# Weight splits of the first 14 chunks on GpSimd instead of ScalarE and VectorE

## Chip, core and metric

The kernel runs on one core of one Trainium2 chip. The core has five engines that run their own instruction queues side by side: TensorE (PE, matrix products), VectorE (DVE), ScalarE (ACT), GpSimd (POOL) and SyncE (SP, which here issues all transfers). The metric is the device time of one execution in microseconds (us); the median of several runs is compared.

## What is computed

Windowed attention over 8 batches and 8 heads (576 positions, 64 numbers per head), then a feed-forward layer with a PReLU in the middle, all float32:

```python
scores = q @ k.T / sqrt(64); masked to 32 positions (half of the heads: every 4th of 128)
attn = softmax(scores);  x = (attn @ v), laid out as 4608 tokens x 512
h = x @ w_in                                   # 512 x 2048
g = np.maximum(h, 0.0) + alpha * np.minimum(h, 0.0)
return g @ w_out                               # 2048 x 512
```

## The kernel before

Matrix products of the feed-forward layer run in a format with fewer bits (fp32r). To keep accuracy, each float32 operand is split in two: a **high** part, the number rounded to fp32r, and a **low** part, the number minus its high part. A product is then three matmuls: high by high, high weight by low activation, low weight by high activation (`PASSES`).

The weights `w_in` and `w_out` come in 32 chunks of 128x512 numbers (16 of each, mostly taken in turn: the list `wq`). The host hands them over as 8-byte numbers, so each chunk is put together on the chip first. The class `Conversion` does it, in steps that the schedule calls one by one:
- `magnitude()`: two instructions on ScalarE (L413, L414) make the tile `wa` (or a spare room with the name `w_2_dt.float_92` or `_93`).
- `words()`: two instructions on VectorE (L421, L423) put in the remaining bits. Both read two tiles in SBUF.
- `high()`: a copy on ScalarE (L429) rounds the chunk into its high part.
- `low()`: a subtraction on VectorE (L432) makes its low part.

The order of instructions on each engine is the order in which the program calls them; nothing reorders them, and each engine works its queue in order. The start of the program is an attention pipeline over pairs of heads (`pairs`), in which the first chunks are converted in the gaps. For one pair: `scores()` (PE, L222 and mask sums L232), `maxima()` (VectorE, L277, L281, later L274), `exponentials()` (ScalarE, nine instructions L287 with their sums), `divisions()` (VectorE, L294, L295 and L296, which multiplies the probabilities `pr` by the broadcast reciprocal sums `rs`, both in SBUF), `turns()` (VectorE transpose L302 into `pt`), `values()` (PE, L317 into `o`), `highs()` (ScalarE, L371) and `lows()` (VectorE, L376), which write high and low parts of the activations `x`. Between them stand a few matmuls on zeros, `idle()` (L126), with no use for the result. The helper `behind()` issues a transfer of one number of a tile, so that the loads after it in SP's queue wait for that tile.

From the fourth pair on, slices of the feed-forward layer of tokens 0 to 511 come in: `ffn_h` (PE, L444, needs the high and low part of a `w_in` chunk), ScalarE's L452, VectorE's L457, ScalarE's L470 (high part of `g`), VectorE's L475 (low part of `g`, from two tiles in SBUF) and `ffn_y` (PE, L492, needs a `w_out` chunk). Chunks 0 and 1 are needed first, by `ffn_h(0, 0, ...)` and `ffn_h(0, 1, ...)`.

GpSimd does nothing in this stage. Later it makes sums of weights in `combine` (L542 on 128x512, L545 on 128x256) while VectorE works on the feed-forward slices.

Of the kernel before, what the change touches and what calls it, by code (L numbers as in the profile page):

```python
# [8 lines left out]
F32 = mybir.dt.float32  # L9
# [25 lines left out]
NFP = NF // 2  # L35
AHEAD = 20
EARLY = 20
GP = 4
GF = 2 * GP
NRING = 10  # L40
# [26 lines left out]
def tile_window_attention_prelu_ffn(  # L67
# [12 lines left out]
    nc = tc.nc  # L80
# [19 lines left out]
    wS = dram.tile([NFP, 7, P, 2, 2 * P], F32, name="wS")  # L100
    wO = dram.tile([NF // GF, NC, GP, P, 2, 2, P], F32, name="wO")
    marks = dram.tile([2 * NC, 1], F32, name="marks")
# [31 lines left out]
    def weight(which, a, f):  # L134
        k = next(k for k in range(3) if f < SPANS[k][1])
        i = 2 * which + a
        if (i, k) not in places:
            places[i, k] = place(i, k)
        return places[i, k][:, f - SPANS[k][0], :]
# [254 lines left out]
    class Conversion:  # L394
# [31 lines left out]

        def high(self):
            self.dst = [weight(self.which, a, self.f) for a in range(2)]
            nc.scalar.copy(out=self.dst[0], in_=self.a.bitcast(F32))  # L429

        def low(self):
            nc.vector.tensor_tensor(  # L432
                out=self.dst[1], in0=self.a.bitcast(F32), in1=self.dst[0].bitcast(F32), op=ALU.subtract)


# [132 lines left out]
    for t in range(NSTD, NTILE, 2):  # L568
        for grp in range(NFP // GP):
            seq = []  # L570
            for i in range(GP):
                seq.append((i, 1))
                if i:
                    seq += [(i - 1, 3), (i - 1, 4)]
                seq += [(i, 7), (i, 6), (i, 2), (i, 5)]
            units += [wS[grp * GP + i, WBLOCK[q]].rearrange("p a n -> p (a n)") for i, q in seq]
            if (t, grp) in SEVENS:
                for i, q in YSTEPS:
                    if q == 0:
                        units += [wS[grp * GP + i, WBLOCK[q]].rearrange("p a n -> p (a n)") for q in (3, 4)]  # L580
                    elif q in YBLOCK:
# [48 lines left out]
    def token_parts(t):  # L630


        k0, k1, z0, z1 = raw(t, 0), raw(t, 1), raw(t + 1, 0), raw(t + 1, 1)

        def diff(out, x, y):
            return lambda: nc.vector.tensor_tensor(out=out, in0=x, in1=y, op=ALU.subtract)

        def high(name, x):
            return lambda: nc.scalar.copy(out=part_of(name, 0), in_=x)

        def low(name, x):
            return lambda: nc.vector.tensor_tensor(
                out=part_of(name, 1), in0=x, in1=part_of(name, 0).bitcast(F32), op=ALU.subtract)

        zeroth = [high("B11", k0), low("B11", k0), high("B21", k1), low("B21", k1)]
        first = [diff(k0, z0, k0), high("T1", k0), low("T1", k0)]
        second = [
            diff(z0, z1, z0), high("T3", z0), diff(k0, z1, k0), high("T2", k0), low("T3", z0),
            diff(k1, k1, k0), low("T2", k0), high("B22", z1), high("T4", k1), low("B22", z1), low("T4", k1),
        ]  # L650
        return zeroth, first, second
# [666 lines left out]
    for p in range(2 * NC, AHEAD):  # L1318
        n = EARLY + 2 * (p - 2 * NC)
        score_at[n] = pairs[p]  # L1320
# [164 lines left out]
```

## Time and profile before

| what | value |
|---|---|
| median of 3 runs | 857.62 us (856.12 to 858.17) |
| the profiled execution's own time | 858.02 us |
| its span | 855.9 us |
| busy in the span: PE, DVE, ACT, POOL | 836.5, 609.6, 435.1, 46.9 us |
| share of the span | 98%, 71%, 51%, 5% |

The span is what the profiler saw from the first to the last instruction; 2.12 us of the execution's own time lie around it. A share is an average over the whole program: PE has 19.4 us without work, and the question in each stage is what it waits for there.

### The profile page before, as it was taken

Reading aid. Unit: us, or ns where it says so; the run is one execution under the profiler, and the core shown is the slowest. Engines: PE = TensorE matmul, PEld = TensorE weight load, DVE = VectorE, ACT = ScalarE, POOL = GpSimd, SP = SyncE. Lnnn points to the kernel's source line nnn. Section 1 sums busy time; section 2 is a strip of 40 time slices with the busy share of each in tenths; the row PEclk is TensorE's granted clock in tenths of the full one; section 3 lists DMA queues with packets and bytes.
Section 4 is the critical chain, followed back from the end, with each engine's and each line's share of the span. In section 5 each row is a group of like instructions: output and inputs, shape, how many; then the busy total and the mean of one; then the engine's idle time right before and its main releaser. Section 6 shows DMA issues by size and latency. Waiting matters only on the chain.

```text
span 855.9 us, 20198 instructions
## 1 busy us (share of the span) xinstructions
PE 836.5 (98%) x8118; PEld 681.7 (80%) x8118; DVE 609.6 (71%) x1047; ACT 435.1 (51%) x1208; POOL 46.9 (5%) x52
## 2 busy tenths in 40 slices
PE   7889999999999999999999999999999999999998
PEld 5677888888888888887778888887888878888886
DVE  5987866766776768678647767777668958834983
ACT  6885766434334444555436543654356426633640
POOL 0000000200505340000000000000000000000000
PEclk9999999999999999999999999999999999999999
DMA  7852444026989963768876577769976776666774
GB/s 250 273 188 97 150 163 148 29 93 201 288 270 322 313 212 129 249 184 254 298 233 196 160 238 250 196 183 300 302 237 191 216 246 198 195 193 193 194 206 140
DMA packets 130746, 179.28 MB, mean 209 GB/s; under 512 B 9822, under 2 KB 74462, under 8 KB 130654
## 3 DMA queue, kind: packets, MB, share of 16 engines
q1 hardware_dynamic: 130654, 178.00, 66.9%
q8 instruction: 64, 1.05, 0.5%
q14 instruction: 28, 0.23, 0.1%
HBM read 136.02 MB, written 41.94 MB: 208 GB/s over the span
## 4 chain that ended last, share of the span: by engine, by line
PE 90%; DVE 4%; DMA 2%; ACT 1%; issue 1%; SPq 0%; ACTq 0%; DVEq 0%
PE h L444 16%; PE y L492 15%; PE pA L657 15%; PE y L909 15%; PE pC L657 7%; PE qA L1029 6%; PE pB L657 4%; PE o L317 3%; PE s L222 2%; PE qC L1029 2%; PE o L264 1%; PE qB L1029 1%; PE s L246 1%; DMA w_dt.float<-qT 1%; DMA v<-vX 1%
## 5 line engine op out<-in xcount | busy, mean ns | idle before, releaser
L444 PE MATMUL h<-x,w_dt.float32r 128*128 128x512 f32 x576 | 142.0, 396 | 0.9 <-ACT x L371 0.8
L492 PE MATMUL y<-g,w_dt.float32r 128*128 128x512 f32 x576 | 138.3, 389 | 0.0
L444 PEld LDWEIGHTS h<-x,w_dt.float32r 128*128 128x128 f32 x576 | 107.7, 189 | 24.0 <-ACT x L371 0.9
L492 PEld LDWEIGHTS y<-g,w_dt.float32r 128*128 128x128 f32 x576 | 108.0, 188 | 22.4
L287 ACT ACTIVATE pr<-pr,nm 128x64 f32<-128x64 f32 x216 | 72.3, 337 | 75.3 <-DVE nm L277 75.3
L470 ACT CAST g<-m 128x512 fp32r<-128x512 f32 x48 | 29.7, 619 | 74.8 <-DVE m L465 71.8
L657 PE MATMUL pA<-parts_w,ring_w 128*128 128x512 f32 x240 | 59.3, 389 | 0.0
L909 PE MATMUL y<-gp,ring_w 128*128 128x512 f32 x240 | 58.2, 394 | 0.0
L657 PE MATMUL pA<-parts_w,ring_xA 128*128 128x512 f32 x234 | 57.8, 389 | 0.0
L909 PE MATMUL y<-gp,ring_xA 128*128 128x512 f32 x228 | 54.9, 394 | 0.0
L657 PEld LDWEIGHTS pA<-parts_w,ring_w 128*128 128x128 f32 x240 | 45.1, 188 | 9.3
L909 PEld LDWEIGHTS y<-gp,ring_w 128*128 128x128 f32 x240 | 44.4, 188 | 9.4
L657 PEld LDWEIGHTS pA<-parts_w,ring_xA 128*128 128x128 f32 x234 | 43.9, 188 | 9.1
L909 PEld LDWEIGHTS y<-gp,ring_xA 128*128 128x128 f32 x228 | 42.2, 188 | 9.1
L475 DVE TENSOR_TENSOR g<-m,g 128x512 fp32r<-128x512 f32 x48 | 33.6, 700 | 15.5 <-ACT g L470 15.4
L699 ACT COPY stage<-pA 128x512 f32<-128x512 f32 x36 | 21.2, 589 | 44.1 <-PE pA L657 43.8
L464 DVE TENSOR_SCALAR m<-h,al 128x512 f32<-128x512 f32 x27 | 20.2, 749 | 29.8 <-PE h L444 29.8
L287 ACT ACTIVATION_READ_ACCUMULATOR pr<-pr,nm 128x1 f32 x216 | 40.7, 189 | 0.0
L713 ACT ACTIVATE n<-stage 128x512 f32<-128x512 f32 x51 | 32.3, 634 | 9.0 <-DVE stage L706 5.8
L793 DVE TENSOR_TENSOR gp<-stage,gp 128x512 fp32r<-128x512 f32 x48 | 32.1, 685 | 2.1 <-ACT gp L789 2.1
L717 DVE SCALAR_TENSOR_TENSOR n<-n,bal,stage 128x512 f32<-128x512 f32 x36 | 27.0, 749 | 6.9 <-ACT n L713 6.4
L725 DVE TENSOR_TENSOR gp<-n,gp 128x512 fp32r<-128x512 f32 x48 | 31.6, 683 | 0.0
(165 smaller groups left out, 1541.2 us busy)
## 6 DMA issues: line engine op xcount, KB each, us to landing
ring_w<-wS SPq DMA_DIRECT2D x67, 256.0 KB, 3.0
ring_xA<-wS SPq DMA_DIRECT2D x67, 256.0 KB, 3.0
ring_w<-wO SPq DMA_DIRECT2D x35, 256.0 KB, 3.0
ring_g<-wS SPq DMA_DIRECT2D x34, 256.0 KB, 2.9
ring_xA<-wO SPq DMA_DIRECT2D x34, 256.0 KB, 2.9
wO<-w_dt.float32r SPq DMA_DIRECT2D x32, 256.0 KB, 4.2
wS<-wc SPq DMA_DIRECT2D x16, 512.0 KB, 4.7
wy<-wO SPq DMA_DIRECT2D x32, 256.0 KB, 5.3
```

The source lines that it names most:

```text
L287: nc.scalar.activation(out=self.pr[:, r, :], in_=self.ps[r // CUT0][:, r % CUT0, :] if self.onto else self.pr[:, r, :], func=AF.Exp, bias= ...
L444: nc.tensor.matmul(ms[t, f], lhsT=weight(0, a, f)[:, c * P:(c + 1) * P], rhs=half(t, c)[:, e, :], start=(c == 0 and n == 0), stop=(c == NC ...
L470: nc.scalar.copy(out=g[:, 0, :], in_=ms[t, f])
L475: nc.vector.tensor_tensor(out=g[:, 1, :], in0=ms.pop((t, f)), in1=g[:, 0, :].bitcast(F32), op=ALU.subtract)
L492: nc.tensor.matmul(ys[t][c], lhsT=weight(1, a, f)[:, c * P:(c + 1) * P], rhs=g[:, e, :], start=(first and n == 0), stop=(last and n == 2),)
L657: nc.tensor.matmul(to, lhsT=w[:, (2 * a + c) * P:(2 * a + c + 1) * P], rhs=part_of(name, e)[:, c * TT:(c + 1) * TT], start=start and c == ...
L713: nc.scalar.activation(out=self.m[n], in_=self.at(n), func=AF.Relu, scale=-1.0)
L717: nc.vector.scalar_tensor_tensor(out=self.m[n], in0=self.m[n], scalar=bal[:, f:f + 1], in1=self.at(n), op0=ALU.mult, op1=ALU.add)
L725: nc.vector.tensor_tensor(out=g[:, 1], in0=self.m.pop(n), in1=g[:, 0].bitcast(F32), op=ALU.subtract)
L793: nc.vector.tensor_tensor(out=p[:, 1], in0=self.whole(n), in1=p[:, 0].bitcast(F32), op=ALU.subtract)
L909: nc.tensor.matmul(ys2[tt], lhsT=w[:, k * P:(k + 1) * P], rhs=g[:, e], start=j == 0 and n == 0, stop=j == GF - 1 and n == 2)
L1029: nc.tensor.matmul(named(to)[c], lhsT=w[:, b * P:(b + 1) * P], rhs=rhs[:, e], start=begins and k == 0, stop=i == GP - 1 and k == 2, skip_g ...
```

## The change

For chunks with an index below `ASIDE` = 14, `high()` is a copy on GpSimd (L431 of the changed kernel) and `low()` a subtraction on GpSimd (L436). The places of the calls in the program, and all other instructions, stay.

```diff
+ASIDE = 14
...
         def high(self):
             self.dst = [weight(self.which, a, self.f) for a in range(2)]
-            nc.scalar.copy(out=self.dst[0], in_=self.a.bitcast(F32))
+            if self.index < ASIDE:
+                nc.gpsimd.tensor_copy(out=self.dst[0], in_=self.a.bitcast(F32))
+            else:
+                nc.scalar.copy(out=self.dst[0], in_=self.a.bitcast(F32))
 
         def low(self):
-            nc.vector.tensor_tensor(
+            (nc.gpsimd if self.index < ASIDE else nc.vector).tensor_tensor(
                 out=self.dst[1], in0=self.a.bitcast(F32), in1=self.dst[0].bitcast(F32), op=ALU.subtract)
```

The changed kernel's lines stand one lower up to L427 and three to four lower behind it (L421 and L423 are L422 and L424 there, L296 is L297, L302 is L303, L376 is L377). On VectorE, in the iteration that ends with the probabilities of the second pair (`pt_1`), these rows stood before; `wa_0_207` is chunk 0, `wa_1_226` chunk 1, `wa_0_254` chunk 2:

```order
L421 SCALAR_TENSOR_TENSOR wa_1_226<-ws_1_108,wa_1_226 128x512
L423 SCALAR_TENSOR_TENSOR wa_1_226<-ws_1_108,wa_1_226 128x512
L432 TENSOR_TENSOR w_0_dt.float32r<-wa_0_207,w_0_dt.float32r 128x512
L277 TENSOR_REDUCE nm_2_341<-s_2_0_258 128x5
L277 TENSOR_REDUCE nm_2_341<-s_2_1_259 128x4
L281 TENSOR_SCALAR nm_2_341<-nm_2_341 128x9
L421 SCALAR_TENSOR_TENSOR wa_0_254<-ws_0_113,wa_0_254 128x512
L423 SCALAR_TENSOR_TENSOR wa_0_254<-ws_0_113,wa_0_254 128x512
```

In the changed kernel VectorE has, at the same place:

```order
L422 SCALAR_TENSOR_TENSOR wa_1_226<-ws_1_108,wa_1_226 128x512
L424 SCALAR_TENSOR_TENSOR wa_1_226<-ws_1_108,wa_1_226 128x512
L278 TENSOR_REDUCE nm_2_341<-s_2_0_258 128x5
L278 TENSOR_REDUCE nm_2_341<-s_2_1_259 128x4
L282 TENSOR_SCALAR nm_2_341<-nm_2_341 128x9
L422 SCALAR_TENSOR_TENSOR wa_0_254<-ws_0_113,wa_0_254 128x512
L424 SCALAR_TENSOR_TENSOR wa_0_254<-ws_0_113,wa_0_254 128x512
```

The low part of chunk 0 is gone from between the words of chunk 1 and the maxima of pair 2. On GpSimd, behind the instructions of the program's start, now stand (the names in front of the arrow are the places of the high and low parts):

```order
L431 CAST w_0_dt.float32r<-wa_0_207 128x512
L431 CAST w_0_dt.float32r<-wa_1_226 128x512
L436 ISA
L436 TENSOR_TENSOR w_0_dt.float32r<-wa_0_207,w_0_dt.float32r 128x512
L431 CAST w_0_dt.float32r<-wa_0_254 128x512
L436 TENSOR_TENSOR w_0_dt.float32r<-wa_1_226,w_0_dt.float32r 128x512
L431 CAST w_0_dt.float32r<-wa_2_370 128x512
L436 TENSOR_TENSOR w_0_dt.float32r<-wa_0_254,w_0_dt.float32r 128x512
L431 CAST w_0_dt.float32r<-w_2_dt.float_92 128x512
L436 TENSOR_TENSOR w_0_dt.float32r<-wa_2_370,w_0_dt.float32r 128x512
L436 TENSOR_TENSOR w_0_dt.float32r<-w_2_dt.float_92,w_0_dt.float32r 128x512
```

The low part of a chunk stands behind the high part of the next one, as it stood before on VectorE behind the words of the next one; the instruction `ISA`, which stood ahead of L542 in the kernel before, now stands ahead of the first subtraction. On ScalarE, the rows between the exponentials of pair 0 and those of pair 1 were

```order
L287 ACTIVATE w_2_dt.float_90,sums_79<-s_0_1_120,nm_0_210 128x64 x4
L429 CAST w_0_dt.float32r<-wa_0_207 128x512
L413 ACTIVATE wa_1_226<-ws_1_108 128x512
L414 ACTIVATE wa_1_226<-wa_1_226,least 128x512
L287 ACTIVATE w_2_dt.float_91,sums_80<-s_1_0_163,nm_1_229 128x64 x5
```

and L429 has left this place and the 13 others like it.

## Rows read from the trace of the kernel before

**Rows 1.** Stretches: length, busy PE, PEld, DVE, ACT, POOL; PE clock, DMA, GB/s.

```profile
18.00:73.00 55.00, 46.76 (x988) 35.83 (x981) 48.99 (x110) 45.33 (x175) 0.00 (x0) 0.97 0.63 213
73.00:164.00 91.00, 91.00 (x404) 75.33 (x403) 65.20 (x101) 56.32 (x96) 1.13 (x1) 1.00 0.35 121
```

**Rows 2.** PE in order of time: start, us, what, [idle before, what ended it].

```profile
23.22 1.35 PE L317 MATMUL o<-pt,w_dt.float 32*64 32x32 f32 x76 [1.05 <-DVE pt L302]
...
28.83 1.48 PE L317 MATMUL o<-pt,w_dt.float 32*64 32x32 f32 x76 [0.92 <-PE idle L126]
30.24 4.37 PE L444 MATMUL h<-x,w_dt.float32r 128*128 128x512 f32 x18
34.55 1.35 PE L317 MATMUL o<-pt,w_dt.float 32*64 32x32 f32 x76
...
48.02 1.70 PE L317 MATMUL o<-pt,w_dt.float 32*64 32x32 f32 x76 [2.18 <-issue]
49.65 4.19 PE L444 MATMUL h<-x,w_dt.float32r 128*128 128x512 f32 x12
...
66.00 1.35 PE L317 MATMUL o<-pt,w_dt.float 32*64 32x32 f32 x76 [1.34 <-issue]
```

**Rows 3.** By line: engine, what, count, ns (least/median/most), first and last start.

```profile
L429 ACT CAST w_dt.float32r<-wa x26: 602/610/692, 12.4 to 157.9; 128x512 fp32r<-128x512 f32 x26
L432 DVE TENSOR_TENSOR w_dt.float32r<-wa,w_dt.float32r x26: 648/685/696, 15.9 to 158.7; 128x512 fp32r<-128x512 f32 x26
L542 POOL TENSOR_TENSOR wsum_xB<-w_dt.float32r x4: 1289/1296/1297, 162.9 to 216.9; 128x512 f32<-128x512 f32 x4
L545 POOL TENSOR_TENSOR wsum_xB<-wsum_xB x8: 730/740/1125, 165.5 to 220.9; 128x256 f32<-128x256 f32 x8
```

**Rows 4.** VectorE in order of time, from chunk 2's words on.

```profile
18.93 0.73 DVE L421 SCALAR_TENSOR_TENSOR wa<-ws,wa 128x512 uint16<-128x512 uint16 x1 [1.40 <-ACT wa L414]
19.70 0.69 DVE L423 SCALAR_TENSOR_TENSOR wa<-ws,wa 128x512 uint32<-128x512 uint32 x1
20.31 0.88 DVE L376 TENSOR_TENSOR x<-o,x 128x288 fp32r<-128x288 f32 x3
...
21.55 0.76 DVE L296 TENSOR_TENSOR w_dt.float<-w_dt.float,rs 128x576 f32<-128x576 f32 x1
...
23.05 0.65 DVE L432 TENSOR_TENSOR w_dt.float32r<-wa,w_dt.float32r 128x512 fp32r<-128x512 f32 x1
23.61 0.81 DVE L277 TENSOR_REDUCE nm<-s 128x5 f32<-128x320 f32 x2
```

**Rows 5.** ScalarE in order of time, between two sets of exponentials.

```profile
16.92 0.66 ACT L429 CAST w_dt.float32r<-wa 128x512 fp32r<-128x512 f32 x1
17.43 0.71 ACT L413 ACTIVATE wa<-ws 128x512 f32<-128x512 bf16 x1
```

**Rows 6.** GpSimd and VectorE in order of time, where both work.

```profile
162.87 2.54 POOL L542 TENSOR_TENSOR wsum_xB<-w_dt.float32r 128x512 f32<-128x512 f32 x2 [162.43 <-PE h L444]
163.61 0.69 DVE L465 SCALAR_TENSOR_TENSOR m<-h,m 128x512 f32<-128x512 f32 x1
164.99 0.97 DVE L475 TENSOR_TENSOR g<-m,g 128x512 fp32r<-128x512 f32 x1 [0.69 <-ACT g L470]
165.49 3.28 POOL L545 TENSOR_TENSOR wsum_xB<-wsum_xB 128x256 f32<-128x256 f32 x4
```

**Rows 7.** VectorE in order of time: chunk 9's words, the last early divisions.

```profile
61.03 0.74 DVE L421 SCALAR_TENSOR_TENSOR wa<-w_dt.uint,wa 128x512 uint16<-128x512 uint16 x1
61.81 0.69 DVE L423 SCALAR_TENSOR_TENSOR wa<-w_dt.uint,wa 128x512 uint32<-128x512 uint32 x1
...
64.33 0.76 DVE L296 TENSOR_TENSOR w_dt.float<-w_dt.float,rs 128x576 f32<-128x576 f32 x1
```

**Rows 8.** A stretch with a lower PE clock, columns as in rows 1.

```profile
50.00:52.00 2.00, 2.00 (x6) 1.52 (x6) 1.97 (x5) 2.00 (x12) 0.00 (x0) 0.50 0.93 375
```

**Rows 9.** GpSimd's configuration instruction, columns as in rows 3.

```profile
L542 POOLq MODIFY_POOL_CONFIG  x2: 11/11/11, 0.7 to 0.8; - x2
```

## The prediction, made before the changed kernel ran

> **What bounds the kernel now.** I read the windows by stage first, since the page's shares average over stages. From 73 to 164 us PE works 91.00 of 91.00 us; from 18 to 73 us it works 46.76 of 55.00 [rows 1]. So whatever the change does there, PE's work behind 73 us only starts earlier or later by what happened before; all the profit must come out of the first 73 us, where PE lacks 8.24 us of work. VectorE has 48.99 us of work in the same 55 us and ScalarE 45.33 [rows 1]: these two feed the attention pipeline and PE waits for them. PE in order of time shows where: the values of a pair (L317) wait 1.05 us for `pt` at 23.22, 0.92 at 28.83, 2.18 at 48.02 and 1.34 at 66.00 [rows 2]; behind 66.00 no such wait is left. One more loss stands behind the wait before 48.02: the granted clock was 0.50 from 50 to 52 us, the lower of the two levels (1.2 GHz) [rows 8], and 12 matmuls took 4.19 us where 18 at 30.24 took 4.37, that is 2.91 for 12; with L317 at 1.70 us against 1.35 this is 1.28 + 0.35 = 1.6 us [rows 2]. The ceiling of any gain is then 8.24 + 1.6 = 9.9 us, 1.15%. About 0.3% (2.6 us) is what a measurement of this kernel can tell from no change.
>
> **What the change takes away.** 14 casts L429 of 0.61 us go from ScalarE and 14 subtractions L432 of 0.685 us from VectorE [rows 3], 8.5 and 9.6 us of busy time. On the path each is worth its distance to the next instruction: 17.43 - 16.92 = 0.51 us on ScalarE [rows 5] and 23.61 - 23.05 = 0.56 us on VectorE [rows 4]. Only those in front of 66.00 count, and only where that engine is what PE waits for.
>
> **What it adds.** GpSimd was idle in this stage [rows 1], so its own time costs nothing unless a weight comes late. The subtraction has the form of L542: two in 2.54 us, 1.27 each [rows 6]. The cast isn't in the trace. Two-input work took 1.296 us for 512 columns and 0.740 for 256 [rows 3], so 256 columns cost 0.556 us and 0.184 is fixed. The cast's bounds are 0.18 (the fixed part alone) and 1.30 (as dear as a subtraction). It reads one input of 512, as much as two inputs of 256 columns, so I take 0.74 and keep both ends.
>
> GpSimd's low parts follow its own queue, not VectorE's, and come at about the old time or earlier; the first matmuls that need them start at 30.24 [rows 2], while chunk 1's words were ready before the old L429 at 16.92 [rows 5]. Weights are therefore not late.
>
> **What it disturbs.** The trace shows that the two engines get into each other's way. L542 ran from 162.87 to 165.41. L475, which reads two tiles in SBUF, was issued at 164.99 and took 0.97 us, though L432, of the same form, takes 0.685 [rows 3, 6]; it ended at 165.96, 0.55 us after GpSimd. So all but the first 0.14 us of it stood still until GpSimd had finished. GpSimd suffers likewise: one L545 took 1.125 us instead of 0.740 [rows 3]. L465, with one input in SBUF and one in PSUM, kept its 0.69 us in the middle of L542 [rows 6]. I conclude that a VectorE instruction with two SBUF inputs waits for a running GpSimd instruction as a whole. In the attention pipeline these are L421, L423 and L296; L376, with one input from PSUM, should run on.
>
> Now one iteration. Chunk 2's words end at t = 19.70 + 0.69 = 20.39 [rows 4]. GpSimd starts 0.08 us behind what it waits for (165.41 to 165.49 [rows 6]), casts until t + 0.82, and its next instruction is chunk 1's subtraction, until t + 2.09. L296 was issued at 21.55 = t + 1.16 [rows 4] and could have gone on at t + 1.30. It is held until t + 2.09: 0.79 us late, and with it the transpose and PE's values. Against that stands the 0.56 us of the L432 gone. Each such iteration is 0.23 us worse.
>
> **The sum**, as shifts of the PE rows [rows 2]:
> - 23.22: chunk 2's words had waited 1.40 us for ScalarE [rows 4]. Two L429 in front of them are gone, so they come 2 x 0.51 = 1.02 us earlier; L296 is held 0.79: -0.23.
> - 28.83: -0.23 - 0.56 + 0.79 = 0.
> - 34.55: again +0.23. PE came to this straight from L444 without a wait, so a little of it may be covered; I take +0.2.
> - 48.02: two more L432 go, but one stood where VectorE waits for exponentials anyway; I count one. The divisions come late enough to miss GpSimd: +0.2 - 0.56 = -0.36.
> - 66.00: two chunks are converted in a row here. Chunk 8's cast becomes ready while L421 of 61.03 runs until 61.77 [rows 7]; GpSimd is next, until 62.51, and L423, which could have gone on at 61.81 + 0.14 = 61.95, is 0.56 late. Its end moves from 62.50 to 63.06, GpSimd casts chunk 9 until 63.88 and subtracts chunk 8 until 65.15. L296 (64.33, plus 0.56, minus 0.56 for the missing L432) could go on at 64.47 and is held 0.68. Sum: -0.36 - 0.56 + 0.56 + 0.68 = +0.32.
>
> PE has no wait behind 66.00 that could take this up, so the profiled execution's 858.02 us become 858.34. The median of the runs is 0.40 us lower, so the forecast is 857.9 us: no change. With the cast at 0.18 every hold is 0.56 shorter (one vanishes) and the shift at 66.00, with PE's own work as a floor at 34.55, comes to about -2.1, 855.5 us; with 1.30, and GpSimd going on to its subtraction without a break, to +3.15, 860.8 us.
>
> The Trainium skill (GPSIMD Engine Reference, 4.1 Engine selection) speaks against the change: elementwise work with two inputs is about twice as slow on GpSimd and belongs on VectorE; with one input it runs at about line rate. The trace agrees on the first half (1.296 against 0.685 us [rows 3]). Line rate at the page's 1.2 GHz would make the cast 0.43 us, an estimate, and by it the sum would be about -1.0 us instead of +0.32, 856.6 us.
>
> The Trainium skill (SBUF — State Buffer, Who interferes with whom) says further that VectorE's tensor_scalar from SBUF to SBUF can block in the same way. No run here shows it. L294 would then also wait, some 0.1 us in each of four iterations, an estimate, and the sum would be near +0.7 us.
>
> **The rivals.**
> 1. Faster: the holds mostly miss. L296 is issued while the cast still runs (cast over about 1.1 us) and takes the port before the subtraction, or the cast is so short that little is left. That L475 went ahead of L545 at 165.41 [rows 6] speaks for the first; against it, the two L542 followed each other without a gap. Without any hold the shifts are -1.02, then -1.58 (at 34.55 PE's own work sets it), -2.14 at 48.02 and -2.7 at 66.00: 854.9 us; if the wait at 48.02 is then short enough for the clock to stay up, 1.6 less, 853.3 us.
> 2. Slower: the cast costs about 1.2 us or more and GpSimd goes straight on to the subtraction. Place: L296 in four iterations, L423 at 61.81. The shift grows from +0.32 at 0.74 to +3.15 at 1.30, and passes 2.6 at about 1.18. Besides, PE's wait at 66.00 would grow past the 2.18 us after which the clock fell at 48.02; another 1.6 us gives 862.4. For it: GpSimd's two-input price. Against it: half the reads.
> 3. Slower: the instruction `ISA`, which becomes MODIFY_POOL_CONFIG, now comes behind chunk 1's cast, with the first subtraction right behind. Before, it ran at 0.7 us and took 0.011 us twice [rows 9], but whatever it started had until 162.87 to finish. Chunk 1's low part is needed by 30.24 + 6 x 0.243 + 0.49 = 32.2, and two subtractions and a cast take 3.3, so the first may start at 28.9; it could start at 16.92 + 0.74 = 17.7. Up to 11.2 us are hidden; a load of 20 us would give 866.
>
> **How the numbers follow.** The forecast, within 0.3% of before, gets 0.58, with a range of its own from 855.5 to 860; rival 1 gets 0.27, rival 2 0.11, rival 3 0.04. Faster is 0.27, same 0.58, slower 0.15. The range from 854.0 to 861.0 takes in most of rival 1 and of the cast's bounds, and leaves out the fall of the clock on top of rival 2, the late load, and rival 1 with the clock kept up.
>
> **What would show it.** PE rows of L317 should stand within 0.4 us of the old starts up to 66.00, and PE should stay without waits from there to 164. VectorE should lose 14 L432 but show its divisions at about 1.5 us instead of 0.76 in the iterations named, and one L423 near 1.25 us. GpSimd's cast should be near 0.74 us. The prediction is wrong if the divisions keep 0.76 us (rival 1), if the cast is over 1.1 us, if PE waits for GpSimd at `h`, or if the clock falls in another place than before: each gap near 2 us decides over 1.6 us.

## The result and the profile after

| | median | runs | mean granted clock of the runs |
|---|---|---|---|
| kernel before, beside it | 858.73 us (856.12 to 862.07) | 6 | |
| changed kernel | 864.03 us (861.78 to 865.50) | 6 | 0.9942 |

The changed kernel is slower: ratio 1.0058, 95% interval 1.0030 to 1.0085. The forecast was no change, 857.9 us, range 854.0 to 861.0. The profiled execution has a span of 863.0 us, 7.1 more than before.

I read the same stretches first. This is the view of windows of the changed kernel: the stage with the change, the next one, and two short stretches inside that the next paragraphs need. Columns: length, busy PE, PEld, DVE, ACT, POOL; PE clock, DMA, GB/s.

```profile
18.00:73.00 55.00, 43.08 (x961) 31.68 (x955) 45.48 (x94) 36.75 (x155) 16.57 (x17) 0.94 0.58 203
73.00:164.00 91.00, 91.00 (x397) 75.18 (x395) 62.23 (x99) 55.99 (x97) 8.37 (x8) 0.98 0.36 126
49.50:52.80 3.30, 3.30 (x4) 1.08 (x4) 2.49 (x7) 2.60 (x9) 0.00 (x0) 0.50 1.03 409
73.40:76.70 3.30, 3.30 (x9) 2.61 (x8) 2.31 (x7) 0.51 (x4) 1.67 (x2) 0.50 0.22 62
```

The two engines that were to be relieved are relieved: VectorE 48.99 to 45.48, ScalarE 45.33 to 36.75 us [rows 1]. PE nevertheless does 3.68 us less in the same 55 us, and behind 73 us it is busy without a break, as before. So all the loss is made ahead of 73 us or in the first microseconds behind it, and part of it at half the clock: the granted clock is 0.50 in the two short stretches here and from 25.6 to 28.9 us; before, it was in one stretch [rows 8]. PE in order of time shows where (start, us, what, [idle before, what ended it]):

```profile
22.97 1.35 PE L318 MATMUL o<-pt,w_dt.float 32*64 32x32 f32 x76 [1.26 <-DVE pt L303]
...
29.57 1.03 PE L318 MATMUL o<-pt,w_dt.float 32*64 32x32 f32 x52
31.83 0.55 PE L318 MATMUL o<-pt,w_dt.float 32*64 32x64 f32 x24 [1.24 <-issue]
32.31 4.38 PE L448 MATMUL h<-x,w_dt.float32r 128*128 128x512 f32 x18
36.62 1.35 PE L318 MATMUL o<-pt,w_dt.float 32*64 32x32 f32 x76
...
43.24 1.04 PE L318 MATMUL o<-pt,w_dt.float 32*64 32x32 f32 x54
47.80 0.54 PE L318 MATMUL o<-pt,w_dt.float 32*64 32x64 f32 x22 [3.52 <-issue]
48.27 1.21 PE L223 MATMUL s<-w_dt.float 64*32 64x64 f32 x72
49.41 3.67 PE L127 MATMUL idle<-pr 128*128 128x512 f32 x4
53.01 0.68 PE L318 MATMUL o<-pt,w_dt.float 32*64 32x32 f32 x29
...
71.60 1.49 PE L318 MATMUL o<-pt,w_dt.float 32*64 32x32 f32 x76 [2.78 <-issue]
73.02 4.60 PE L448 MATMUL h<-x,w_dt.float32r 128*128 128x512 f32 x12
```

Beside the old starts [rows 2] the values come 0.25 us earlier, then 0.74, 2.07, 4.99 and 5.60 us later. Behind the last one `h` takes 4.60 us at a granted clock of 0.50 instead of 3.02 (the same 12 matmuls at 63.08), 1.58 more: 5.60 + 1.58 = 7.18, the whole difference of the spans (7.1). What the reader should note besides: stops of PE marked "issue" stand in the middle of a group (52 matmuls, a stop, 24 matmuls; 3.52 us behind 44 us), where the profile shows nothing that is waited for. The step from 2.07 to 4.99 us lies around the stop of 3.52 us, and no VectorE instruction is held there; other profiles of the same work show 1.24 (e1) and 2.09 us (e12) at this place, so that step belongs in part to this execution. The 2.78 us ahead of the last values are marked "issue" too, but they end 0.10 us behind VectorE's transpose (L303, until 71.50): this is a wait for VectorE.

Now the question of the prediction: which VectorE instruction is held? VectorE in order of time, the first two iterations and the one of the last values:

```profile
16.46 1.26 DVE L282 TENSOR_SCALAR nm<-nm 128x9 f32<-128x9 f32 x1
...
19.80 1.21 DVE L295 TENSOR_SCALAR rs<-sums 128x9 f32<-128x9 f32 x1
...
21.30 0.76 DVE L297 TENSOR_TENSOR w_dt.float<-w_dt.float,rs 128x576 f32<-128x576 f32 x1
...
25.87 1.22 DVE L295 TENSOR_SCALAR rs<-sums 128x9 f32<-128x9 f32 x1
...
27.38 0.76 DVE L297 TENSOR_TENSOR w_dt.float<-w_dt.float,rs 128x576 f32<-128x576 f32 x1
...
67.70 1.18 DVE L295 TENSOR_SCALAR rs<-sums 128x9 f32<-128x9 f32 x1
...
69.17 1.52 DVE L297 TENSOR_TENSOR w_dt.float<-w_dt.float,rs 128x576 f32<-128x576 f32 x1
```

and GpSimd beside them:

```profile
15.75 0.62 POOL L431 CAST w_dt.float32r<-wa 128x512 fp32r<-128x512 f32 x1 [3.93 <-DVE wa L424]
16.41 1.28 POOL L436 TENSOR_TENSOR w_dt.float32r<-wa,w_dt.float32r 128x512 fp32r<-128x512 f32 x1
19.15 0.61 POOL L431 CAST w_dt.float32r<-wa 128x512 fp32r<-128x512 f32 x1 [1.46 <-DVE wa L424]
19.72 1.27 POOL L436 TENSOR_TENSOR w_dt.float32r<-wa,w_dt.float32r 128x512 fp32r<-128x512 f32 x1
25.23 0.61 POOL L431 CAST w_dt.float32r<-wa 128x512 fp32r<-128x512 f32 x1 [4.24 <-DVE wa L424]
25.80 1.27 POOL L436 TENSOR_TENSOR w_dt.float32r<-wa,w_dt.float32r 128x512 fp32r<-128x512 f32 x1
...
67.56 1.29 POOL L436 TENSOR_TENSOR w_dt.float32r<-w_dt.float,w_dt.float32r 128x512 fp32r<-128x512 f32 x1
68.81 1.25 POOL L436 TENSOR_TENSOR w_dt.float32r<-wa,w_dt.float32r 128x512 fp32r<-128x512 f32 x1
```

The multiplication L297, which the prediction named, keeps its 0.76 us in the first two iterations. Held is L295 in front of it, an addition to nine numbers per partition with one input (0.16 us otherwise, median over all 32). It was issued at 19.80, 0.08 us behind the start of the subtraction at 19.72, and ended at 21.01, 0.02 us behind the subtraction's end at 20.99; the same at 25.87, and with L282 (0.17 us otherwise) at 16.46. Ahead of the last values two subtractions follow each other, and two instructions are held: L295 by the first of them, about 1.0 us, and L297 by the second, 0.76 us.

### The profile page after: what moved, and what is told of

The parts are those of the page before. It is cut to its first block, busy times and chain, and to the rows that moved or that the text cites. A ratio compares the mean times of both kernels' runs of the same rounds, so it can differ in the third digit from the quotient of the medians.

```text
span 863.0 us, 20234 instructions
## 1 busy us (share of the span) xinstructions
PE 840.5 (97%) x8118; PEld 683.6 (79%) x8118; DVE 608.4 (71%) x1033; ACT 428.5 (50%) x1194; POOL 74.4 (9%) x80
## 4 chain that ended last, share of the span: by engine, by line
PE 89%; DVE 4%; DMA 2%; ACT 2%; issue 1%; SPq 0%; ACTq 0%
PE h L448 16%; PE y L496 15%; PE pA L661 15%; PE y L913 14%; PE pC L661 7%; PE qA L1033 6%; PE pB L661 4%; PE o L318 3%; PE qC L1033 2%; PE s L223 2%; PE o L265 1%; PE qB L1033 1%; PE s L247 1%; DMA w_dt.float<-qT 1%; PE idle L127 1%
```

## The experiments

Theory P (the port): the holds of VectorE by GpSimd's subtractions are the loss. Rivals: C, the falls of PE's clock; I, PE's stops for its instructions; D, work that comes earlier on VectorE and ScalarE does harm by itself. Each run is compared with the kernel before on the same chip.

**The changed kernel again, and its halves.** The first is the changed kernel itself. The second leaves the subtractions on VectorE, the third leaves the casts on ScalarE.

```diff
# e2, in low()
-            (nc.gpsimd if self.index < ASIDE else nc.vector).tensor_tensor(
+            nc.vector.tensor_tensor(
# e3, in high()
-            if self.index < ASIDE:
+            if False:
```

> The changed kernel as it is, once more. Port theory (VectorE waits for whole GpSimd instructions, and the short tensor_scalar of the divisions waits first): the same seven holds of 0.5 to 1.1 us on L282, L295 and L297 in front of the last early values, time again about 0.6% over before. Supply theory (PE stops in the middle of a pair's values, 1.2, 3.5 and 0.5 us, because its instructions are late, and this has nothing to do with GpSimd's port): the holds are there too, but the stops in PE have other lengths in this execution, and the time scatters by some 3 us with them.

Measured: 862.40 us, 1.0046 (1.0029 to 1.0063), mean clock 0.9947 where the kernel before had 0.9980 over its 29 runs. The loss repeats; L295 takes 1.03 to 1.17 us at three places, and L297 1.55 and 1.52 us at two.

> Only the 14 casts on GpSimd, the subtractions on VectorE as before. Port theory: a cast of 0.61 us that starts 0.08 us behind the words ends while VectorE is in L377, which doesn't need the port, so no hold over 0.2 us; ScalarE is 0.51 us lighter per chunk; time 0 to 1.5 us below before. Supply theory: PE's stops stay as in the changed kernel, time 2 to 6 us above before.

Measured: 859.86 us, 1.0009 (0.9994 to 1.0025), clock 0.9965. No L295 is held; one L424 takes 0.94 us instead of 0.69.

> Only the 14 subtractions on GpSimd, the casts on ScalarE as before. Port theory: a subtraction now starts behind ScalarE's cast, not behind the words, so it meets other VectorE instructions: fewer holds on L295 than in the changed kernel, but some; time between before and the changed kernel, 0 to 3 us above before. Supply theory: PE's stops as in the changed kernel, 2 to 6 us above before.

Measured: 861.21 us, 1.0029 (1.0010 to 1.0048), clock 0.9948. L295 takes 1.30 us at 62.80, L297 1.69 and 1.52. By the medians the subtractions alone give most of the loss (2.8 of 4.0 us, though the intervals of e1 and e3 overlap); the casts alone give nothing that can be told from no change.

**Subtractions behind the divisions, first try.** A copy of one column on GpSimd, which needs the divisions' result, goes ahead of each subtraction, into a tile of its own; in the later loop the calls of `low()` move behind the divisions.

```diff
+    gate, divided_last = const.tile([P, 1], F32, name="gate"), []
...
+                nc.gpsimd.tensor_copy(out=gate, in_=divided_last.pop()[:, HB - 1, BK - 1:])
```

> Casts and subtractions on GpSimd, but each subtraction (and from the loop over slices on each cast) waits for the divisions of the pair, by a copy of one column of the probabilities, so that it runs beside the transpose and the maxima, which don't need the port. Port theory: L295 and L297 keep 0.17 and 0.76 us in all iterations; VectorE is 0.56 us lighter per iteration and nothing is given back; time 1 to 3 us below before. Supply theory: as the changed kernel, 2 to 6 us above before.

Measured: 871.62 us, 1.0149 (1.0125 to 1.0173). The holds are nearly gone and the last values start at 66.07 as in the kernel before, but 12 matmuls take 2.96 us everywhere, not 2.88. Something else had been changed, and the next three runs look for it: the tile 32 times as wide, the kernel before with such a tile and nothing else (one memset on GpSimd), and the kernel before once more.

> As the kernel with the subtractions behind the divisions, but the helper tile takes 128 bytes of a partition instead of 4, so that all tiles behind it keep their place modulo 128 bytes. If the 2.96 us per 12 matmuls seen there (2.88 elsewhere) came from the shifted addresses, it is 2.88 again. Port theory: L295 and L297 keep 0.17 and 0.76 us in the iterations named, time 1 to 3 us below before. Supply theory: PE still stops at the same three places in the middle of a pair's values, which take back what VectorE gains, time within 1 us of before or above it.

> The kernel before with one more tile of 4 bytes per partition, set by one memset on GpSimd, and nothing else. If addresses shifted by 4 bytes slow PE, 12 matmuls take 2.96 us instead of 2.88 and the time is 1.2 to 1.7% over before (868 to 873 us). If the slow matmuls came from GpSimd's work, the time is that of before.

> The kernel before in a second profiled execution. Port theory: nothing to show, all tensor_scalars at 0.17 us. Supply theory: PE's stops at the block places differ from those of the first profile (0.4 and 1.2 us before 20 us, none at the three later places), by up to some us, without any change in the kernel.

Measured: 871.03 us, 1.0145 (1.0119 to 1.0171); 873.98 us, 1.0168 (1.0144 to 1.0192); 860.26 us in one run. The added tile, with its memset, costs 1.7%, and these tries say nothing of theory P. The kernel before with the tile, its window behind the stage (columns as above):

```profile
73.00:164.00 91.00, 91.00 (x391) 73.10 (x390) 64.31 (x99) 55.83 (x96) 0.00 (x0) 1.00 0.36 120
```

and PE in order of time in it:

```profile
92.40 2.96 PE L495 MATMUL y<-g,w_dt.float32r 128*128 128x512 f32 x12
```

391 matmuls in 91 us, where 404 fitted before [rows 1], at the full clock in both.

**The split work left out, first try.** The tiles of the first 14 chunks are filled once, by four memsets of 128x4096 on GpSimd.

```diff
+         nc.gpsimd.memset(places[i, 0].bitcast(F32), 0.015625)
...
+            if self.index >= ASIDE:
                 nc.scalar.copy(out=self.dst[0], in_=self.a.bitcast(F32))
```

> High and low parts of the first 14 chunks aren't made at all: the four weight tiles are filled once with a constant by GpSimd at the start of the program, and the products use that. This is the ceiling of any move of this work: VectorE 9.6 and ScalarE 8.5 us lighter, GpSimd's port free from 20 us on. Port theory: the time falls by 2 to 4 us below before. Supply theory: PE stops at the block places as in the changed kernel and the time falls by less than 2 us or not at all.

Measured: 864.04 us, 1.0050 (1.0031 to 1.0069), clock 0.993. As slow as the changed kernel with nothing of the work left: I took theory P for refuted and looked to C and I. That was wrong, as the run e11 below shows.

**More matmuls on zeros, to keep PE at work**, in the changed kernel, in the kernel before and in the one without the split work.

```diff
-            idle(f"a{(2 * s + 1) % 4}", 3 - s)
+            idle(f"a{(2 * s + 1) % 4}", 4 - s)
...
-            idle("y0", n + 1)
+            idle("y0", 2 * n + 1)
+            idle("y0", 1 - n, 256)
+        if n == 2:
+            tag = f"a{turn['a'] % 4}"
+            idle(tag, 1)
+            idle(tag, 1, 256)
```

> The changed kernel with 5 us more of matmuls on zeros in front of the values of five pairs (1 us more at 20, 28, 50 and at 70, half a us more at 43 and at 70), where the changed kernel's PE stands still for 2 to 3.5 us in all. Theory C (the clock): the mean granted clock of the changed kernel's runs was 0.994, of the kernel before 0.998, so it loses nearly two more stretches of 3.4 us at half the clock; with PE kept at work the mean clock comes back to 0.997 or more and the time falls from 862.4-864.0 to 858-860. Theory P (the port): VectorE's holds set PE's waits, idle matmuls only fill them; the clock may come back, but the waits in front of the last values stay as long in sum and the time stays at 861 or above. Theory I (PE's instruction supply alone): stops in the middle of a group get shorter by what the idle matmuls in front of them take, and the sum stays: 861 to 865.

> The kernel before with the same 5 us of matmuls on zeros. It loses little to the clock (0.998), and its waits in these places are 1.05, 0.92, 0, 2.18 and 1.34 us, so some of the added work lies on the path. Theory C: clock 0.999 or more, time 857 to 860, ratio 0.999 to 1.002. Theories P and I: the idle work that is longer than a wait is added, 1 to 2 us: 859 to 861.

> The kernel in which the high and low parts of the first 14 chunks are not made at all (four tiles filled once with a constant instead, the output is not the reference's), with the same 5 us of matmuls on zeros. Without them it took 864.0 at a mean clock of 0.993. Theory C: clock 0.997 or more and 857 to 860, that is 4 us or more faster than without the idle matmuls, since there is nothing else in it that is slower than in the kernel before. Theory I: the same time as without them, 862 to 866.

Measured: changed 861.62 us, 1.0034 (1.0020 to 1.0048), clock 0.9980; before 858.01 us, 1.0000 (0.9980 to 1.0020), clock 0.9992; without the split work 863.44 us, 1.0062 (1.0037 to 1.0086). The clock of the changed kernel is back, and it still takes 3.6 us more than the kernel before with the same idle matmuls: the clock by itself is not the whole loss. The profiles of the first two are both at the full clock (1.00) through these stages, so their iterations can be laid side by side. VectorE's transposes, which PE's values wait for, in the changed kernel with more idle matmuls:

```profile
21.80 0.78 DVE L303 STREAM_TRANSPOSE pt<-w_dt.float 128x576 f32<-128x576 f32 x1
...
27.87 0.78 DVE L303 STREAM_TRANSPOSE pt<-w_dt.float 128x576 f32<-128x576 f32 x1
...
34.76 0.78 DVE L303 STREAM_TRANSPOSE pt<-w_dt.float 128x576 f32<-128x576 f32 x1
```

and in the kernel before with the same idle matmuls:

```profile
21.33 0.78 DVE L302 STREAM_TRANSPOSE pt<-w_dt.float 128x576 f32<-128x576 f32 x1
...
26.94 0.78 DVE L302 STREAM_TRANSPOSE pt<-w_dt.float 128x576 f32<-128x576 f32 x1
...
33.36 0.78 DVE L302 STREAM_TRANSPOSE pt<-w_dt.float 128x576 f32<-128x576 f32 x1
```

They come 0.47, 0.93 and 1.40 us later: about 0.47 more in each iteration. In the first two L295 takes 1.22 us instead of 0.16, 1.06 more, and the missing L432 gives 0.56: 0.50. That is the price of a hold, read without the clock. At the last values (67.18 against 65.33) the difference is 1.85 us; a further 2.3 us of the two spans (859.8 and 855.6) arise behind 250 us, among them a stop of PE of 1.12 us in the middle of `h` at 280 and one of 0.66 at 305, which I can't tie to the change. Stops of 0.48 to 1.44 us stand at 303 to 307 us in three other kernels with these idle matmuls (e11, e15, e16) and in none without them. So the 3.6 us are not all the price of the holds.

The run without the split work shows at its start why it was slow. GpSimd in order of time:

```profile
0.73 13.86 POOL L144 MEMSET w_dt.float32r<- 128x4096 f32 x4 [0.29 <-POOLq L1487]
```

and VectorE beside it:

```profile
8.72 5.89 DVE L283 TENSOR_SCALAR nm<-nm 128x9 f32<-128x9 f32 x1
9.17 5.44 DVE L423 SCALAR_TENSOR_TENSOR wa<-ws,wa 128x512 uint16<-128x512 uint16 x1
```

My own memsets held VectorE until they ended at 14.59, 5.9 us in this execution (2.95 and 1.96 us at two places in e8). One memset takes 3.51 us: the hold went on over the end of the third into the fourth. The experiment had put in what it was to take out.

**Fewer loads**, to see whether PE's instructions come late because the weight loads are in the way.

```diff
+        if not 2 * NC <= i < 2 * HALF:
             nc.sync.dma_start(out=halves[:, :4 * DM - 1], in_=src.bitcast(U16)[:, 1:])
```

> The changed kernel in which the loads of chunks 8 to 15 (8 of 32, 4.2 MB) are left out; their conversion reads what lies in the four staging rooms from chunks 4 to 7, so the output is not the reference's. All engines do the same work. Theory I, in the form that PE's instruction blocks come late because they queue behind the weight loads: the stops in the middle of PE's groups between 43 and 72 us (3.52, 0.48, 2.78 in the changed kernel, 1.24, 0.46, 2.77 in its second look) shrink to under half, the last values start at 67 or earlier, and the time falls to 857-860. Theories C and P: the stops depend on what PE and VectorE do, not on the loads: the time stays within 1.5 us of 862.4-864.0.

Measured: 862.45 us, 1.0039 (1.0019 to 1.0058), clock 0.9944. The stop inside the group of values at 42 us is still 2.09 us. The 2.77 us ahead of the values at 68 us end 0.10 us behind VectorE's transpose and say nothing of theory I. Theory I in this form falls.

**Theory P, with the two faults mended.** The gate's column now goes into the tile that the subtraction overwrites next, so no tile is added (`low()` stands behind the divisions as in e4); the kernel without the split work is filled by four copies of 128x512 at the start, and its 14 chunks share that slice. Each was run without and with the additional idle matmuls.

```diff
# e13 and e16
+            divided_last[:] = [self.pr]
...
+            while self.index < ASIDE and divided_last:
+                nc.gpsimd.tensor_copy(out=self.dst[1][:, :1], in_=divided_last.pop()[:, HB - 1, BK - 1:])
# e14 and e15
+        if order.get((which, f), ASIDE) < ASIDE:
+            f = 0
...
+        nc.gpsimd.tensor_copy(out=places[i, 0][:, 0, :], in_=pairs[0].k[:, :DM])
```

> The changed kernel with each subtraction on GpSimd put behind the last divisions of VectorE, by a copy of one column of the probabilities into the tile that the subtraction then overwrites; no tile is added, so all addresses stay. Theory P (VectorE's holds by the subtractions set the loss): no L295 or L297 over 1.0 us up to 66 us, PE's values at 35 to 66 us come 1 us or more earlier than in the changed kernel, time 857 to 860 against 862.4-864.0. Rival D (what comes earlier on VectorE and ScalarE does harm by itself, by loads or stops of PE): holds gone, time still 861 or above.

> High and low parts of the first 14 chunks are not made; all matmuls read one slice, filled once at the start with numbers of k by four short copies on GpSimd (output not the reference's). Theory P: nothing holds VectorE, and 14 subtractions and 14 casts are gone from it and ScalarE: 854 to 858, at or under the kernel before. Rival D: 861 or above, as with the long memsets (864.0).

> The kernel of the run before with the 5 us of matmuls on zeros in front of five pairs' values. Theory P: clock 0.999 or more and 854 to 858. Rival D: 861 or above. If the first 73 us are limited by PE's own work and the idle matmuls once nothing else is, it is no faster than the kernel before with the same idle matmuls (858.0).

> The changed kernel with the subtractions behind the divisions and the 5 us of matmuls on zeros. Without the gate it took 861.6 at a clock of 0.998, the kernel before with the same idle matmuls 858.0. Theory P: 857 to 859. Rival D: 860.5 to 862.5, as without the gate.

Measured: gated 858.23 us, 0.9990 (0.9975 to 1.0006), clock 0.9974; without the split work 858.51 us, 0.9991 (0.9977 to 1.0005), clock 0.9972; the latter with more idle 859.52 us, 1.0002 (0.9987 to 1.0017); the former with more idle 858.93 us, 0.9997 (0.9981 to 1.0013). All four come back to the kernel before. In the gated kernel VectorE shows the holds gone from the first two iterations:

```profile
19.71 0.16 DVE L295 TENSOR_SCALAR rs<-sums 128x9 f32<-128x9 f32 x1
...
25.12 0.16 DVE L295 TENSOR_SCALAR rs<-sums 128x9 f32<-128x9 f32 x1
```

since GpSimd's gate and subtraction now come behind them:

```profile
21.06 0.19 POOL L438 CAST w_dt.float32r<-w_dt.float 128x1 fp32r<-128x1 f32 x1 [1.38 <-DVE w_dt.float L297]
21.32 1.27 POOL L439 TENSOR_TENSOR w_dt.float32r<-wa,w_dt.float32r 128x512 fp32r<-128x512 f32 x1
```

The same 14 subtractions and casts on the same engine, the subtraction only 1.6 us later in the iteration, and the 4 us are gone, the lower clock of the runs with them (0.9947 to 0.9974). Holds are left where they cost little: one L295 takes 0.85 us at 34.25, and behind the last divisions, where PE has no more wait for VectorE, the words of a chunk take 1.15 and 1.63 us instead of 0.74 and 0.69. PE's stops in the middle of groups stay (1.55 and 2.13 us), so they are not the loss. Theory P stands; rival D falls.

Where most of the loss arises is seen at the last values and the `h` behind them, in the changed kernel run again (e1):

```profile
68.64 1.55 PE L318 MATMUL o<-pt,w_dt.float 32*64 32x32 f32 x76 [2.77 <-issue]
70.11 4.59 PE L448 MATMUL h<-x,w_dt.float32r 128*128 128x512 f32 x12
```

and in the gated kernel:

```profile
66.09 1.55 PE L319 MATMUL o<-pt,w_dt.float 32*64 32x32 f32 x76 [0.75 <-issue]
67.57 3.04 PE L451 MATMUL h<-x,w_dt.float32r 128*128 128x512 f32 x12
```

In the four profiles with ungated subtractions and no added idle matmuls (the changed kernel, e1, e3, e12) PE waits 2.63 to 2.78 us there and `h` takes 4.36 to 4.60 us, at a granted clock of 0.50. In the kernel before (both profiles), e2, e13 and e14 the wait is 0.75 to 1.60 us and `h` takes 3.02 to 3.04. Against the kernel before (1.34 and 3.02) that is 2.6 to 3.0 us in this one place, about half of it wait and half of it clock. So the clock is no cause beside the holds here: at this place it falls only behind the wait that the two holds have made longer.

That 14 casts and 14 subtractions fewer bring nothing either is the other half of the finding. PE in the kernel without them:

```profile
22.13 1.35 PE L321 MATMUL o<-pt,w_dt.float 32*64 32x32 f32 x76 [0.37 <-DVE pt L306]
...
27.27 1.03 PE L321 MATMUL o<-pt,w_dt.float 32*64 32x32 f32 x52
30.63 0.86 PE L321 MATMUL o<-pt,w_dt.float 32*64 32x64 f32 x24 [2.33 <-issue]
31.43 5.59 PE L448 MATMUL h<-x,w_dt.float32r 128*128 128x512 f32 x18
...
66.29 1.35 PE L321 MATMUL o<-pt,w_dt.float 32*64 32x32 f32 x76 [0.76 <-issue]
```

PE is 1.09 us ahead at the first values and 1.56 at the second [rows 2], and then stands still for 2.33 us inside that group; `h` starts 1.19 us later than in the kernel before, partly at the lower clock (5.59 us against 4.37), and the last values start at 66.29 against 66.00.

**The stops moved.** So the place of these stops was shifted by 52 matmuls, in the gated kernel and in the kernel before.

```diff
-    idle("a3", 2)
+    idle("a3", 2, 256)
+    narrow = psp.tile([P, TT], F32, tag="a3", name="idle_narrow")
+    for _ in range(26):
+        nc.tensor.matmul(narrow[:32, :32], lhsT=pr0[:, 0, :32], rhs=pr0[:, 0, :32], start=True, stop=True)
```

> The kernel with the gated subtractions (858.2) in which the third pair of matmuls on zeros is half as wide and 26 narrow ones (52 records on PE) follow it, so that each place where PE stops for its instructions comes 52 matmuls earlier in the program: the stop inside the values at 28 and 42 us (52 and 54 matmuls, then 24 and 22) comes to stand in front of the group, where PE waits for the transpose anyway. Theory I (these stops take back what the missing work on VectorE and ScalarE gives): no stop inside these two groups, the values end 1 to 2 us earlier at 30, time 855.5 to 857.5. Rival (PE's stops are only another name for the wait for VectorE and ScalarE): the group moves, the time stays at 857.5 to 859.5.

> The kernel before with the same move of the places of PE's stops. In its profile the stops inside these two groups are short or missing (28.83: 0.1 us; in a second look 1.36). Theory I: 0 to 1.5 us faster, 857 to 859.5 beside 858.6. Rival: no change within 0.5 us.

Measured: 857.63 us, 0.9996 (0.9980 to 1.0012), and 858.08 us, 0.9985 (0.9969 to 1.0001). The stops left the middle of the two groups of values and came back at other places (in the kernel before one of 0.72 us stands behind the first matmul of a group); in the gated kernel:

```profile
45.57 0.98 PE L223 MATMUL s<-w_dt.float 64*32 64x64 f32 x54
49.76 0.49 PE L223 MATMUL s<-w_dt.float 64*32 64x64 f32 x18 [3.20 <-issue]
```

Their place moves with the count of PE's instructions, as theory I has it, but the time doesn't move by more than the measurement can tell. What sets the length of these stops, and with it why the stage can't be made shorter, stays open. No kernel here is shown to be faster than the kernel before.

## Why the prediction was wrong, step by step

- **The removed work** was priced rightly as far as it goes. The shift at 23.22 without any hold was put at 1.02 us and measured 1.09 (e14), that at 28.83 at 1.58 and measured 1.56. But the step "VectorE and ScalarE feed the pipeline and PE waits for them" failed behind that: rival 1 forecast 854.9 us without holds, 3.1 less than before, and 858.5 was measured, 1.1 less than before on that chip and not clear of no change. The 0.92 to 2.18 us in front of PE's values are not all VectorE's and ScalarE's to give back; in e14 a stop of PE marked "issue" (2.33 us) and a stretch at the lower clock took the gain within the next group.
- **The added work**: the subtraction at 1.27 us was measured at 1.28, the cast, put at 0.74, at 0.61. The estimate from the Trainium skill (GPSIMD Engine Reference, 4.1 Engine selection), 0.43 by line rate, was too low; the trace's 0.61 is what ScalarE took for the same copy [rows 3]. Weights were not late.
- **The failing step** is "In the attention pipeline these are L421, L423 and L296", with the 0.79 us that followed from it. The conclusion that a VectorE instruction waits for a running GpSimd instruction as a whole was right; that it takes two inputs was drawn from one example, L475 [rows 6], which could not show it. Held were also L294 (L295 after) and L281 (L282 after), with one small input, and the prediction's path has no term for them. Because the cast is 0.13 us shorter than put, the subtraction starts just ahead of L295 (19.72 and 19.80), and the hold has nearly its full length: 1.06 instead of 0.79 us, and the balance of an iteration is +0.50 instead of +0.23. Ahead of the last values the forecast hold of L296 (L297 after) came, 0.76 us for 0.68; the hold of L295 in front of it, about 1.0 us, came on top. With it PE's wait there grew to 2.78 us, and the clock fell.
- The prediction cited the rule that would have said so: the Trainium skill (SBUF — State Buffer, Who interferes with whom) lets VectorE's tensor_scalar from SBUF to SBUF block too. The traces now agree, with up to 1.30 us where the prediction allowed 0.1 us in each iteration. It had given the rule to the cast's time alone and not asked what the subtraction behind the cast would do to an instruction issued 0.08 us later.
- **The shifts**: forecast -0.23, 0, +0.2, -0.36, +0.32; in the profile -0.25, +0.74, +2.07, +4.99, +5.60. The first agrees by luck: the 1.02 us gained ahead of it were eaten by L282's hold of 1.09. At the full clock (e9 against e10) they are +0.34, +0.46, +0.69, +0.58, +1.85: the largest step, 1.27 us, is that of the last iteration, for which the prediction had 0.68. The hold of L423 at 61.81 was forecast (0.56 us longer) and came as 0.25 (0.94 to 0.95 against 0.69).
- **The clock** was named as a danger ("each gap near 2 us decides over 1.6 us"), and 1.58 us is what the fall behind 71.60 cost, after a wait of 2.78 us. The prediction had a fall at this place only on top of rival 2, outside its range, and none behind a hold of L294. Over the runs the clock fell to 0.994 on the mean, and gating the subtractions brought it back to 0.997. At the last values the clock's part is 1.3 to 1.6 us (`h` at 4.36 to 4.60 instead of 3.02). For the whole loss it stays open: the idle matmuls raised the clock to 0.998, and the ratio went from 1.0046 to 1.0034, within both intervals.
- **Rival 3** fell: the two MODIFY_POOL_CONFIG took 0.011 us each, and the first subtraction started at 16.41 right behind the cast. (Its sum should read 866.7: 20 - 11.2 = 8.8 us over 857.9.)
- PE had no wait from the last values on to 164 us, as forecast.

## What to carry to other kernels

An engine with idle time is no free place for work if its instructions hold those of the engine that sets the pace: ask of each of that engine's instructions in the same few microseconds, the tiny ones with one input too, whether it could be issued while the added instruction runs, and price it at the added instruction's whole length (where GpSimd's instructions follow each other without a break it can be more: 5.89 us beside memsets of 3.51). Ask also what follows the longest wait that results; here the lower clock came on top. If the work must move, gate it to where the pacing engine's instructions are not held; here that was beside the transpose (0.78 us as before) and the maxima, 1.6 us later in the iteration, and it turned a loss of 0.46% into none. And before relieving an engine, run the kernel with the work left out: if that isn't faster, nothing that hides the work should be expected to be; but see that the kernel that leaves it out brings no disturbance of its own.

## What the runs showed of the hardware that was not expected

- A VectorE instruction on 128x9 numbers with one input, 0.16 us by itself, was held until GpSimd's instruction ended: it took up to 1.30 us beside subtractions and 5.89 us beside memsets, which only write. The last is longer than one memset (3.51 us).
- A 128x512 cast on GpSimd took 0.61 us, no more than on ScalarE, and held nearly nothing (e2: one instruction, by 0.25 us). Up to 73 us most casts of e2 ran beside L377, with one input in PSUM, or the maxima; the three that met L422 or L436, with two inputs in SBUF, took 1.01 to 1.09 us themselves.
- One added tile of 4 bytes per partition, used by nothing else, made 12 matmuls of 128x512 take 2.96 us instead of 2.88 in the feed-forward part, at the same granted clock, and cost 1.7%; 128 bytes did much the same (2.94 to 2.96 us in e5). Not every operand was hit: later matmuls `pA` that stream `ring_xA` took 395 ns instead of 389 on the mean, those with `ring_w` 390 and 389. That the cause is the addresses of the tiles behind the added one wasn't tried.
- PE stops for 0.2 to 3.5 us in the middle of groups of small matmuls; adding 52 matmuls at the start moved the places. With 4.2 MB of weight loads left out, a stop of 2.09 us stayed (1.24 and 3.52 us at this place with them).
